# A gated mix of a long convolution and an MLP mixer: layer norm 2 as centred squares, full-height matmuls for the D term, and a new order

## The chip, the cores and the metric

The kernel runs on one core of a Trainium2 chip. The metric is the device time in microseconds (us) of one execution; the figure for a kernel is the median over its runs. A core has five engines with a program each: TensorE (PE, matmuls; its weight loads are listed as PEld), VectorE (DVE), ScalarE (ACT), GpSimd (POOL) and SyncE (SP, which here issues the DMAs). They run side by side and wait for one another through semaphores.

## The reference

With S = 2048 tokens, D = 640 and F = 1536, all in bfloat16, the output mixes two branches of the same input q:

```python
def reference(A_q, A_k, A_v, A_shift_k, A_ssm_k, A_ssm_D, B_x, B_w1, B_w2, B_w3, B_w4, gate_w):
    x = A_q
    g = sigmoid((x * gate_w).sum(-1, keepdims=True))
    # branch a: short convolution of k (4 taps), times v, long convolution over the sequence
    k_shift = sum_t k_pad[:, t:t + S, :] * shift_k[:, 3 - t]
    kv = k_shift * v
    y = irfft(rfft(kv, padded to 2 S) * rfft(ssm_k, padded to 2 S))[:S]     # per channel
    a = q * (y + kv * ssm_D)
    # branch b: two layer norms with an MLP each
    h = gelu(layernorm(x) @ w1)                 # layernorm: (x - mean) / sqrt(var + 1e-5)
    hs = (four column groups of h, shifted by 1, -1, 2, -2 tokens) @ w2
    x1 = x + hs
    b = x1 + gelu(layernorm(x1) @ w3) @ w4
    return g * a + (1 - g) * b
```

## The kernel before

The 2048 tokens are held as 16 slabs of 128 (partition p of slab t is token 16 p + t), and `QX[:, s, :]` holds slab s of q, later of x1, and at last of the output. Names of steps below are those of the plan, followed by slab or chunk numbers.

Branch b: `st0`, `rs0` and `xn0` are layer norm 1 (statistics, reciprocal root on GpSimd, normalised slab on VectorE). `xt` transposes a slab into `XNT` by DMA (`tr` does it by TensorE for the first slabs). `W1.c.n` is the first matmul for chunk c of four slabs (L586), `g1` its gelu on ScalarE (L593), `mx` the copies that shift the remainders of the column groups (L621 to L626). `W2.s` (L675) and `add s` (L682, VectorE) give x1; the add also sums each row into `SSM`. Layer norm 2 is `st1.s` (one square on ScalarE with a row sum into `SSQ`, L515), `rs1.s` on GpSimd for a pair of slabs (L531 to L535: mean, its square, subtraction, epsilon, power -0.5) and `xn1.s` on VectorE. `W3.c.f` (L761), `g2` (gelu, L765), `W4.s.j` (L774) and `w4e` (L780, VectorE) follow. The gate is `z` and `gate0` (VectorE), `gate1` (tanh on ScalarE, L648), `gate2`; `xo` scales x1 by 1 - g.

Branch a: the long convolution is done in two steps of a transform, through DRAM. Step 1 of the filter is `h1.s.h` (L730), evicted as `he` into staging and written by `hw` to `GHD`; the filter comes in as `h0` to `h4` and is transposed by `trh`. At slab 0 each of these two steps also adds the D term, the product of a row of ones and zeros (`ONE1`) with D (`DROW`), a matmul of one row (L733). `ka`, `kb`, `kc`, `k1` to `k3` load k and `v0` to `v3` load v (L807). VectorE forms kv by products (`km`, L823) and sums (`ka.`, L827), and `kv s` multiplies by v for two slabs (L830). `x1.s.h`, `xe`, `xw` are step 1 for kv, written to `GXD`. `rh` and `rx` read the two back in another order (L874), `h2` and `x2` are step 2 as 64-wide matmuls (L847), `sw` swaps real and imaginary parts (two DMAs), `pq` multiplies (L907, VectorE), `pv` transforms back, `vw` writes to `VD`, `rv` reads, `iv s` (L943) is the last step, `y` and `ya` form g * q * y and add it to `QX`, and `st s` stores a slab. `rq` loads q again.

`m3i`, `m3b`, `m3c`, `m3d`, `m3s`, `m3n` build the matrices of step 2: iotas and `m3c` (L444 to L460) on GpSimd, `m3d` (L464) on VectorE, the sine `m3s` (L466) on ScalarE, `m3n` on GpSimd.

The order of all the work is written out: `ORDER` is a text of 789 entries such as `W2.9/P/2`, which give a step, its engine (P TensorE, V VectorE, A ScalarE, G GpSimd, S SyncE's DMA queue) and the slots of the buffers it uses (banks of PSUM, staging areas). Each engine does its own entries in the order of the text. `Plan.add` takes for each step a time per engine; the text was made with them, and once it is written they have no effect on the program. PSUM has eight banks of 512 floats, and a step that needs a bank waits until the one before in that bank has been evicted.

Of the kernel before, what the change touches and what calls it, by code (L numbers as in the profile page):

```python
# [9 lines left out]
ACT = mybir.ActivationFunctionType  # L10
# [75 lines left out]
bpi/V is/G cs/V iw/G cw/V ang3/V and3/V sin3.1/A q1/S idn/G h0/S ang1/V ang2/V and1/V st0.2/V sin1.1/A abs1/A q0/S st0.1/A  # L86
st0.3/V warm/P/0 trh0/P/2 trhe0/A/2 h4/S trh4/P/4 st0.0/V ang0/V and0/V sin0.1/A h1/S trh1/P/6 trhe1/A/6 sin1.0/A rs0.2/G
xn0.2/V/0 xn0.3/V/1 tr0.0.2/P/0/0/0/1 trhe4/V/4 rs0.0/G misc/G xn0.1/V/2 xn0.0/V/0 h3/S trh3/P/2 abs0/A sin0.0/A and2/V
te0.0.2/V/0/0 sin2.1/A tr0.0.0/P/4/0/0/2 te0.0.0/V/4/0 q3/S st0.7/V st0.6/V w1/S W1.0.3/P/0/0 W1.0.2/P/1/0 w1m/G q2/S st0.4/A
trhe3/V/2 st0.5/V h2/S trh2/P/6 g1.0.3/A/0 g1.0.2/A/1 W1.0.0/P/2/0 g1.0.0/A/2 trhe2/V/6 W1.0.4/P/3/0 g1.0.4/A/3 h1.5.0/P/4/0  # L90
h1.1.1/P/6/1 he.1.1/A/6/1 rs0.6/G xn0.6/V/1 xn0.7/V/0 tr0.1.2/P/0/1/1/0 q7/S q4/S q5/S st0.10/A rs0.4/G xn0.4/V/2 q6/S gw/S
gt.0/P/2/0 w2b3/S he.5.0/V/4/0 h1.4.0/P/4/0 he.4.0/A/4/0 xn0.5/V/0 te0.1.2/V/0/1 tr0.1.0/P/6/1/2/0 te0.1.0/V/6/1 z0/V/2
h1.3.1/P/0/2 st0.11/V he.3.1/A/0/2 W1.0.1/P/3/0 h1.5.1/P/6/0 g1.0.1/A/3 w2b2/S he.5.1/A/6/0 h1.3.0/P/4/2 he.3.0/A/4/2
W1.1.4/P/2/1 h1.4.1/P/0/0 he.4.1/A/0/0 g1.1.4/A/2 W1.1.1/P/3/1 h1.1.0/P/6/1 g1.1.1/A/3 he.1.0/A/6/1 h1.2.1/P/4/2 he.2.1/A/4/2
w2b1/S w2a/S w2b0/S W1.1.2/P/2/1 drow/S kc/S/0 ka/S/0 h1.0.1/P/0/1 he.0.1/A/0/1 h1.0.0/P/6/1 he.0.0/A/6/1 cjb/S g1.1.2/A/2
W1.1.3/P/3/1 st0.9/V h1.2.0/P/4/2 he.2.0/A/4/2 g1.1.3/A/3 hw2/S/0 W1.1.0/P/0/1 g1.1.0/A/0 mx0.1/G rs0.10/G st0.8/V rs0.8/G
xn0.10/V/1 xt0.2.2/S/0/1 st0.15/V xn0.11/V/0 st0.14/V xt0.2.3/S/0/0 rs0.14/G mx0.2/V xn0.9/V/2 st0.12/V mx0.0/V mx1.3/G
st0.13/V gt.1/P/1/1 xn0.8/V/1 z1/V/1 hw0/S/1 xt0.2.1/S/0/2 h1.7.0/P/6/0 h1.7.1/P/4/0 v0/S he.7.0/V/6/0 xt0.2.0/S/0/1 abs3/A
xn0.15/V/0 xt0.3.3/S/1/0 W2.2/P/2 sin3.0/A add2/V/2 abs2/A he.7.1/A/4/0 h1.6.0/P/0/0 st1.2/A he.6.0/V/0/0 mx1.1/G W2.4/P/6
add4/V/6 sin2.0/A m3i1/G xn0.14/V/2 kb/S/0 hw1/S/2 W2.3/P/2 add3/V/2 h1.13.0/P/0/1 he.13.0/V/0/1 h1.6.1/P/4/0 he.6.1/A/4/0  # L100
rs0.12/G xt0.3.2/S/1/2 kz/V/0 xn0.12/V/1 xn0.13/V/0 mx1.0/G W2.5/P/6 hw3/S/0 xt0.3.1/S/1/0 xt0.3.0/S/1/1 add5/V/6 h1.12.1/P/2/1
gt.2/P/0/0 he.12.1/A/2/1 h1.12.0/P/4/1 he.12.0/V/4/1 W1.2.1/P/1/0 st1.4/A st1.3/A g1.2.1/A/1 m3i2/G m3i0/G m3i3/G mx1.2/G cj1/G
m3i5/G v1/S h1.13.1/P/2/1 he.13.1/V/2/1 mx0.3/G cj0/G hw6/S/1 W1.2.2/P/6/0 cj3/G z2/V/0 h1.8.1/P/4/2 he.8.1/A/4/2 m3i4/G
W1.2.4/P/0/0 st1.5/A W1.2.3/P/1/0 g1.2.3/A/1 h1.10.1/P/2/0 he.10.1/A/2/0 h1.10.0/P/4/0 he.10.0/A/4/0 g1.2.4/A/0 W1.2.0/P/7/0
g1.2.0/A/7 km0.0.3/V/0/0 h1.9.0/P/2/2 m3b/V he.9.0/A/2/2 g1.2.2/A/6 W1.3.0/P/1/1 h1.8.0/P/4/2 he.8.0/A/4/2 cj2/G km0.0.2/V/0/0
km0.0.1/V/0/1 ka0.0.2/V/0/0 rs1.2/G xn1.2/V/2 xt1.0.0/S/0/2 ka0.0.1/V/1/0 xn1.3/V/0 km0.0.0/V/0/0 gt.3/P/0/1 z3/V/0
ka0.0.0/V/0/0 kv0/V/0 h1.11.1/P/2/0 he.11.1/A/2/0 W1.3.1/P/6/1 g1.3.1/A/6 h1.9.1/P/4/2 he.9.1/A/4/2 g1.3.0/A/1 W1.3.3/P/0/1
h1.14.1/P/2/1 h1.15.0/P/6/1 he.15.0/A/6/1 he.14.1/A/2/1 h1.14.0/P/4/1 he.14.0/A/4/1 W1.3.4/P/1/1 g1.3.4/A/1 g1.3.3/A/0
W1.3.2/P/6/1 g1.3.2/A/6 w3/S h1.11.0/P/2/0 he.11.0/A/2/0 km0.1.3/V/0/0 rs1.4/G xn1.4/V/1 xt1.0.1/S/0/0 xt1.0.2/S/0/1 xn1.5/V/2
xt1.0.3/S/0/2 mx2.3/V gate0/V mx2.1/G W2.7/P/4 mx2.0/G km0.1.2/V/0/1 km0.1.1/V/0/0 ka0.1.2/V/1/0 ka0.1.1/V/0/0 m3c/G m3d/V  # L110
m3s/A m3n/G k1/S/1 mx2.2/G mx3.1/V km0.1.0/V/0/1 mx3.0/G ka0.1.0/V/1/0 W2.6/P/0 add6/V/0 add7/V/4 W2.8/P/6 add8/V/6 gate1/A
gate2/V kv2/V/0 W2.9/P/2 add9/V/2 km1.0.3/V/1/0 km1.0.2/V/1/0 km1.0.1/V/1/1 W3.0.1/P/0/0/0 g2.0.1/A/0/0 ka1.0.2/V/0/0 mx3.3/G
km1.0.0/V/1/0 ka1.0.1/V/1/0 ka1.0.0/V/0/0 kv4/V/0 xo5/A st1.6/A st1.8/A st1.9/A rs1.8/G xn1.9/V/0 k2/S/0 w4/S v2/S
km1.1.3/V/1/0 W3.0.4/P/1/0/1 W3.0.11/P/0/0/2 hw5/S/0 g2.0.11/A/0/2 g2.0.4/A/1/1 km1.1.2/V/1/1 ka1.1.2/V/1/0 xn1.8/V/1
km1.1.1/V/1/0 ka1.1.1/V/0/0 xt1.1.2/S/1/1 hw4/S/2 tri0/S xo2/V h1.15.1/P/4/1 v3/S km1.1.0/V/1/1 ka1.1.0/V/1/0 st1.7/A
he.15.1/A/4/1 rs1.6/G xn1.7/V/2 W3.0.6/P/2/0/1 W3.0.5/P/3/0/1 g2.0.5/A/3/1 g2.0.6/A/2/1 kv6/V/0 W2.11/P/6 W3.0.7/P/0/0/1
add11/V/6 xt1.1.1/S/1/2 km2.0.3/V/0/0 km2.0.2/V/0/0 W3.0.0/P/1/0/0 W3.0.8/P/2/0/2 g2.0.8/A/2/2 g2.0.0/A/1/0 xn1.6/V/1
xt1.1.0/S/1/1 xt1.1.3/S/1/0 W3.0.9/P/3/0/2 g2.0.9/A/3/2 xo4/A W3.0.3/P/2/0/0 W3.0.2/P/1/0/0 g2.0.7/A/0/1 g2.0.3/A/2/0 xo3/A
g2.0.2/A/1/0 ka2.0.2/V/0/0 W3.0.10/P/0/0/2 W2.10/P/4 km2.0.1/V/0/1 add10/V/4 ka2.0.1/V/1/0 km2.0.0/V/0/0 ka2.0.0/V/0/0 kv8/V/0
g2.0.10/A/0/2 W4.3.1/P/0/0/1/2 w4e3.1/V/0 W4.5.1/P/1/0/1/2 W4.5.0/P/2/0/1/2 W4.2.1/P/3/0/1/2 x1.2.0/P/6/0 W4.3.0/P/4/0/1/2  # L120
xe.2.0/A/6/0 km2.1.3/V/0/0 w4e3.0/V/4 km2.1.2/V/0/1 st1.11/A W2.13/P/6 w4e5.1/V/1 w4e2.1/V/3 W4.4.0/P/0/0/1/2 w4e5.0/V/2
W2.12/P/4 w4e4.0/V/0 add12/V/4 st1.10/A ka2.1.2/V/1/0 km2.1.1/V/0/0 W4.2.0/P/0/0/1/2 st1.12/A W3.1.10/P/1/1/3 w4e2.0/V/0
add13/V/6 km2.1.0/V/0/1 ka2.1.1/V/0/0 ka2.1.0/V/1/0 kv10/V/0 hw7/S/1 k3/S/1 tri1/S mx3.2/G rs1.10/G xn1.11/V/2 xt1.2.1/S/0/2
x1.3.1/P/2/0 xe.3.1/A/2/0 st1.13/A g2.1.10/A/1/3 rs1.12/G km3.0.3/V/1/0 km3.0.2/V/1/0 ka3.0.2/V/0/0 km3.0.1/V/1/1 x1.3.0/P/4/0
xe.3.0/A/4/0 W3.1.8/P/0/1/3 g2.1.8/A/0/3 xn1.13/V/1 ka3.0.1/V/1/0 km3.0.0/V/1/0 ka3.0.0/V/0/0 x1.2.1/P/6/0 xe.2.1/A/6/0
kv12/V/0 xw1/S/0 W4.4.1/P/2/0/1/2 w4e4.1/V/2 x1.0.1/P/4/2 xe.0.1/A/4/2 x1.0.0/P/0/2 xe.0.0/A/0/2 W3.1.1/P/3/1/0 g2.1.1/A/3/0
x1.6.1/P/6/1 xe.6.1/A/6/1 W3.1.7/P/0/1/1 g2.1.7/A/0/1 x1.1.1/P/4/2 x1.1.0/P/6/2 W3.1.9/P/1/1/3 xe.1.0/A/6/2 xe.1.1/A/4/2
x1.7.1/P/6/1 xe.7.1/A/6/1 g2.1.9/A/1/3 W3.1.0/P/0/1/0 g2.1.0/A/0/0 xt1.2.3/S/0/1 xw0/S/2 x1.7.0/P/4/1 xe.7.0/A/4/1 x1.6.0/P/6/1
xe.6.0/A/6/1 xw3/S/1 xn1.12/V/0 xn1.10/V/2 km3.1.3/V/1/0 xt1.2.0/S/0/2 xt1.2.2/S/0/0 W3.1.3/P/1/1/0 g2.1.3/A/1/0 km3.1.2/V/1/1
ka3.1.2/V/1/0 km3.1.1/V/1/0 xo12/V ka3.1.1/V/0/0 km3.1.0/V/1/1 ka3.1.0/V/1/0 kv14/V/0 x1.9.1/P/4/0 x1.8.0/P/2/0 xe.8.0/A/2/0  # L130
xe.9.1/A/4/0 W3.1.4/P/0/1/1 g2.1.4/A/0/1 x1.9.0/P/6/0 xe.9.0/A/6/0 W3.1.2/P/1/1/0 g2.1.2/A/1/0 x1.8.1/P/2/0 xe.8.1/A/2/0
xw4/S/0 x1.12.0/P/4/2 xe.12.0/A/4/2 x1.13.0/P/6/2 xe.13.0/A/6/2 W3.1.5/P/0/1/1 x1.13.1/P/2/2 xe.13.1/A/2/2 x1.12.1/P/4/2
xe.12.1/A/4/2 xw6/S/2 W3.1.11/P/1/1/3 g2.1.11/A/1/3 x1.10.1/P/6/1 x1.10.0/P/2/1 xe.10.0/V/2/1 xe.10.1/V/6/1 xo7/A W2.14/P/4
g2.1.5/A/0/1 W2.1/P/2 add14/V/4 rh0/S/0 x1.4.1/P/0/0 x1.5.1/P/6/0 xe.5.1/A/6/0 add1/V/2 W2.0/P/4 rh1/S/1 x1.15.0/P/2/2 st1.1/A
xe.15.0/A/2/2 add0/V/4 st1.0/A xe.4.1/V/0/0 W3.1.6/P/6/1/1 xo9/V rs1.0/G x1.11.1/P/4/1 xe.11.1/A/4/1 st1.14/A x1.4.0/P/2/0
W3.2.1/P/7/0/2 g2.2.1/A/7/2 xe.4.0/A/2/0 xo8/V x1.11.0/P/0/1 xe.11.0/V/0/1 xw5/S/1 W2.15/P/4 x1.14.0/P/0/2 xe.14.0/V/0/2
add15/V/4 x1.5.0/P/2/0 xe.5.0/A/2/0 xw2/S/0 W3.2.3/P/7/0/2 g2.1.6/A/6/1 xn1.0/V/1 x1.15.1/P/0/2 xe.15.1/V/0/2 g2.2.3/A/7/2
x1.14.1/P/2/2 xe.14.1/A/2/2 xw7/S/2 st1.15/A rs1.14/G xt1.3.2/S/1/1 rq0/S/0 W3.2.0/P/6/0/2 h2.1.1/P/4/1/0 h2e.1.1/A/4/0
g2.2.0/A/6/2 h2.1.4/P/2/1/0 h2e.1.4/V/2/0 h2.1.3/P/0/1/0 W3.2.2/P/7/0/2 h2e.1.3/V/0/0 h2.1.0/P/4/1/0 h2.0.3/P/2/0/1
h2e.0.3/A/2/1 h2e.1.0/V/4/0 g2.2.2/A/7/2 W4.8.1/P/6/0/1/3 h2.1.2/P/0/1/0 h2e.1.2/V/0/0 w4e8.1/V/6 h2.0.0/P/2/0/1 h2.0.1/P/4/0/1  # L140
# [39 lines left out]
def kernel(  # L180
# [322 lines left out]
    def ln_slab(i, s, dep):  # L503
        s0 = s & ~1

        def f_st(e):
# [4 lines left out]
            else:  # L511
                if i == 0:
                    nc.scalar.activation(out=JNK if i else JN0, in_=QX[:, s, :], func=ACT.Copy, scale=1.0 / D,
                                         accum_out=MV[:, i, s, 0:1])
# [485 lines left out]
```

## Time and profile before

| | us |
|---|---|
| median of 4 runs (lowest, highest) | 230.19 (229.45, 231.22) |
| the profiled execution's own time | 230.35 |
| its span | 228.6 |
| TensorE busy | 214.7 (94%) |
| VectorE busy | 189.7 (83%) |
| ScalarE busy | 162.6 (71%) |
| GpSimd busy | 62.1 (27%) |
| DMA: 65.90 MB | mean 288 GB/s |

The span is the time from the first to the last recorded piece of the execution; the rest of its time lies around it. The page also cuts the span into 40 slices of 5.7 us; each digit is the busy share in tenths (9 is 90% or more), and PEclk is the TensorE clock that was granted:

```profile
PE   6869999999789999999999999999989999999990
DVE  8998989989599999999976878888869887027993
ACT  5999979899677713199967863698982987616760
POOL 2653469699858403260002200000000000000000
PEclk9999999999979999999999999999999999999999
```

The chain that ended last is followed back from the last instruction: at each step to what released it, or to the instruction before on its engine. In a group's line stand the line of code, engine, operation, output and input, shapes, the count, then busy time and the mean in ns of one, then the idle time of the engine ahead of them and what ended most of it.

### The profile page before, as it was taken

To read this page: it belongs to the slowest core of one execution; us is meant where nothing else is said; L and a number is where in the kernel's file an instruction comes from. 1 tells how busy PE (TensorE), PEld (TensorE's weight loads), DVE (VectorE), ACT (ScalarE), POOL (GpSimd) and SP (SyncE) were. 2 spreads that over 40 slices of the span, in tenths; PEclk is the share of its full clock that TensorE was granted. 3 is DMA by queue.
4 is the path that set the end of the run, shared out by engine and by line. 5 is a ranking of instruction groups with operands and counts; after the bars stand their busy time and mean duration, and the time that the engine had idled before them with its cause. 6 is when DMAs were issued, how large, how long until landed. Compare 5 with 4: busy or idle time off the path is not lost.

```text
span 228.6 us, 4449 instructions
## 1 busy us (share of the span) xinstructions
PE 214.7 (94%) x1641; PEld 125.1 (55%) x1641; DVE 189.7 (83%) x347; ACT 162.6 (71%) x250; POOL 62.1 (27%) x133
## 2 busy tenths in 40 slices
PE   6869999999789999999999999999989999999990
PEld 6737557555535477655575456533335554457770
DVE  8998989989599999999976878888869887027993
ACT  5999979899677713199967863698982987616760
POOL 2653469699858403260002200000000000000000
PEclk9999999999979999999999999999999999999999
DMA  7999999999999499909999989999997973889985
GB/s 214 383 394 248 313 256 197 296 265 362 285 330 364 167 230 243 301 11 193 302 292 372 351 246 373 247 297 372 358 377 230 391 292 136 287 297 397 394 288 180
DMA packets 53030, 65.90 MB, mean 288 GB/s; under 512 B 22544, under 2 KB 39697, under 8 KB 52624
## 3 DMA queue, kind: packets, MB, share of 16 engines
q1 hardware_dynamic: 53008, 65.61, 92.5%
q8 instruction: 13, 0.21, 0.4%
q14 instruction: 9, 0.07, 0.1%
HBM read 37.03 MB, written 18.35 MB: 242 GB/s over the span
## 4 chain that ended last, share of the span: by engine, by line
PE 61%; DMA 12%; DVE 10%; POOL 7%; issue 3%; SPq 2%; ACT 1%; ACTq 0%; DVEq 0%; POOLq 0%
PE PS L774 18%; PE PS L761 16%; PE PS L675 7%; PE PS L847 6%; DMA RG<-in_A_ssm_k_dram 5%; PE PS L730 5%; DMA RK<-GHD 4%; PE PS L586 4%; PE PS L943 4%; DMA R<-R 3%; POOL MV L531 2%; DVE RK L827 2%; DVE RK L823 2%; DVE QX L682 1%; POOL RS L535 1%
## 5 line engine op out<-in xcount | busy, mean ns | idle before, releaser
L332 ACT CAST SX<-PS 128x640 bf16<-128x640 f32 (+1 forms) x65 | 47.7, 764 | 25.4 <-PE PS L730 13.3
L761 PE MATMUL PS<-XNT,W 128*128 128x512 bf16 x240 | 58.2, 388 | 2.1 <-DVE QX L682 2.1
L774 PE MATMUL PS<-W,RG 128*128 128x320 bf16 x384 | 56.0, 299 | 0.6 <-ACT RG L765 0.6
L774 PEld LDWEIGHTS <-RG 128*128 128x128 bf16 x384 | 36.5, 98 | 19.6 <-issue 4.7
L761 PEld LDWEIGHTS <-W 128*128 128x128 bf16 x240 | 23.1, 100 | 30.5 <-issue 8.5
L765 ACT ACTIVATE RG<-PS 128x512 bf16<-128x512 f32 x48 | 27.5, 604 | 6.6 <-PE PS L761 6.3
L907 DVE TENSOR_TENSOR SX<-SX,R 128x2048 bf16<-128x2048 bf16 x20 | 24.3, 1221 | 3.5 <-ACT SX L332 2.2
L780 DVE SCALAR_TENSOR_TENSOR QX<-PS,ZG,QX 128x320 bf16<-128x320 f32 x32 | 16.9, 545 | 11.1 <-PE PS L774 10.9
L586 PE MATMUL PS<-XNT,R 128*128 128x512 bf16 x100 | 24.2, 379 | 1.0 <-DMA R<-in_B_w_dram 1.0
L730 PE MATMUL PS<-KV,F 128*128 128x320 bf16 x128 | 24.9, 299 | 0.1
L675 PE MATMUL PS<-R 128*128 128x320 bf16 x160 | 23.5, 299 | 0.0
L336 DVE CAST SX<-PS 128x640 bf16<-128x640 f32 (+1 forms) x19 | 18.1, 966 | 3.5 <-PE PS L730 1.9
L827 DVE TENSOR_TENSOR RK<-RK 128x1280 bf16<-128x1280 bf16 x24 | 19.8, 826 | 0.4
L332 ACT CAST KV<-PS 128x1024 bf16<-128x1024 f32 x18 | 18.0, 1025 | 2.1 <-PE PS L847 2.0
L823 DVE TENSOR_TENSOR RK<-RK,CJ 128x1280 bf16<-128x1280 bf16 x24 | 19.4, 817 | 0.0
L675 PEld LDWEIGHTS <-R 128*128 128x128 bf16 x160 | 15.7, 98 | 6.4
L531 POOL TENSOR_SCALAR MV<-ST 128x2 f32<-128x2 f32 x8 | 7.2, 904 | 39.5 <-DVE QX L682 39.2
L730 PEld LDWEIGHTS <-F 128*128 128x128 bf16 x128 | 12.2, 98 | 9.7 <-issue 0.3
L586 PEld LDWEIGHTS <-R 128*128 128x128 bf16 x100 | 9.6, 98 | 10.5 <-DMA R<-in_B_w_dram 1.2
L515 ACT ACTIVATE RG<-QX 128x640 bf16<-128x640 bf16 x16 | 11.8, 737 | 4.7 <-issue 4.6
L682 DVE SCALAR_TENSOR_TENSOR QX<-PS,QX 128x640 bf16<-128x640 f32 x16 | 12.9, 818 | 2.4 <-PE PS L675 2.3
L847 PEld LDWEIGHTS <-M 64*64 64x64 bf16 x320 | 7.5, 105 | 12.9 <-issue 7.0
(110 smaller groups left out, 292.2 us busy)
## 6 DMA issues: line engine op xcount, KB each, us to landing
GHD<-SX SPq DMA_DIRECT2D x8, 640.0 KB, 4.6
GXD<-SX SPq DMA_DIRECT2D x8, 640.0 KB, 4.2
RK<-GHD SPq DMA_DIRECT2D x4, 1280.0 KB, 8.6
RK<-GXD SPq DMA_DIRECT2D x4, 1280.0 KB, 7.5
R<-R SPq DMA_DIRECT2D x8, 640.0 KB, 7.5
VD<-KV SPq DMA_DIRECT2D x4, 1280.0 KB, 7.2
W<-in_B_w_dram SPq DMA_DIRECT2D x2, 1920.0 KB, 9.5
RK<-in_A_k_dram SPq DMA_DIRECT2D x3, 1120.0 KB, 6.0
```

The source lines that it names most:

```text
L332: nc.scalar.copy(out=o, in_=i)
L336: nc.vector.tensor_copy(out=o, in_=i)
L586: nc.tensor.matmul(ps(pb), lhsT=lhsT, rhs=XNT[:, xb.idx, k, :], start=(k == 0), stop=(k == DT - 1))
L675: nc.tensor.matmul(ps(pb)[:, j, 0:DH], lhsT=gst_ap(k, s), rhs=W2[:, k, j * DH:(j + 1) * DH], start=(k == 0), stop=(k == DT - 1))
L730: nc.tensor.matmul(ps(pb)[:, j, 0:DH], lhsT=F1[:, s // 4, h, s % 4, :], rhs=src[:, s, ds], start=True, stop=not dterm)
L761: nc.tensor.matmul(ps(pb), lhsT=W3[:, k, f0 * P:(f0 + 1) * P], rhs=XNT[:, xb.idx, k, :], start=(k == 0), stop=(k == DT - 1))
L765: gns.append(pl.add("g2.%d.%d" % (c, f0), {A: act_p(512)}, lambda e, f0=f0, pb=pb, gb=gb: nc.scalar.activation(out=GTP[:, gb.idx, f0 % 4, ...
L774: nc.tensor.matmul(ps(pb)[:, 0:DH], lhsT=GTP[:, gbs[f // 4].idx, f % 4, i * P:(i + 1) * P], rhs=W4[:, f, j * DH:(j + 1) * DH], start=(f == ...
L823: m = pl.add("km%d.%d.%d" % (c, u, j), {V: dve(2 * D, .52)}, lambda e, src=src, cj=cj, tb=tb: nc.vector.tensor_tensor(out=TMP[:, tb.idx].r ...
L827: prev = pl.add("ka%d.%d.%d" % (c, u, j), {V: dve(2 * D, .52)}, lambda e, tb=tb: nc.vector.tensor_tensor(out=acc, in0=acc, in1=TMP[:, tb.i ...
L847: nc.tensor.matmul(pt[64 * C:64 * C + 64, R, :], lhsT=M3[64 * R:64 * R + 64, m, :], rhs=rhs_fn(R, C), start=start, stop=stop)
L907: nc.vector.tensor_tensor(out=PQ[:, qb.idx], in0=XS[:, sb.idx].unsqueeze(1).to_broadcast([P, 2, 1024]), in1=HH[:, hhb.idx, u], op=ALU.mult)
```

## The change

1. Layer norm 2: `st1.s` on ScalarE is now a copy of one column, `SSM * (-1/D)` into `MV` (the negated mean), and then a square of x1 with that as its bias and the row sum into `SSQ`. The second waits for the first. `rs1` on GpSimd is then two instructions in place of five, and `xn1` adds the negated mean instead of subtracting the mean.
2. The D term: `ONE1` becomes 128 x 128, zero except for its first row; `DROW` holds D on all 128 partitions, loaded by a broadcast (160 KB in place of 1.2 KB). The matmuls of L733 then have 128 rows.
3. Times of the plan: `m3c` 5000 to 7000 ns, `st1` 735 to 930, `rs1` 2300 to 1900, the first two `h1` doubled.
4. `ORDER` is another text throughout, with the same 789 steps: order on each engine, slots of buffers, and the engine of some (21 from VectorE to ScalarE and 16 the other way, nearly all evictions; `kz`, `mx0.0`, `mx2.3`, `mx3.1` from VectorE to GpSimd, `mx1.0` back). The table loads of ScalarE become eight, from seven: the gate's tanh now stands between gelus. Of the DMA queue: `v0` is issued after `xt0.3.0` (before: ahead of `xt0.2.0`), `rq0` after `rh2`, `rq1` and `rq2` late.

```diff
-    ONE1 = big.tile([1, P], BF16, name="ONE1")
+    ONE1 = big.tile([P, P], BF16, name="ONE1")
...
-    DROW = W34[0:1, 14700:14700 + D]
-    lddr = pl.dma("drow", lambda e: nc.sync.dma_start(out=DROW, in_=A_ssm_D.rearrange("(o d) -> o d", o=1)), D * 2, ldq, ndesc=1)
+    DROW = W34[:, 14700:14700 + D]
+    lddr = pl.dma("drow", lambda e: nc.sync.dma_start(out=DROW, in_=A_ssm_D.partition_broadcast(P)), P * D * 2, [ldq[-1]], ndesc=128)
...
-    m3c = pl.add("m3c", {G: 5000}, f_m3c, m3a)
+    m3c = pl.add("m3c", {G: 7000}, f_m3c, m3a)
...
         nc.gpsimd.memset(ONE1[:], 0.0)
-        nc.gpsimd.memset(ONE1.rearrange("p (j c) -> p j c", c=2)[:, :, 0:1], 1.0)
+        nc.gpsimd.memset(ONE1[0:1, :].rearrange("p (j c) -> p j c", c=2)[:, :, 0:1], 1.0)
...
+                else:
+                    nc.scalar.activation(out=MV[:, i, s, 0:1], in_=SSM[:, s:s + 1], func=ACT.Copy, scale=-1.0 / D)
+                    nc.scalar.activation(out=JNK, in_=QX[:, s, :], func=ACT.Square, bias=MV[:, i, s, 0:1],
+                                         accum_out=SSQ[:, s:s + 1])
...
+                if i == 1:
+                    ve = VE[:, i, s0:s0 + 2]
+                    g.tensor_scalar(out=ve, in0=SSQ[:, s0:s0 + 2], scalar1=1.0 / D, scalar2=1e-5, op0=ALU.mult, op1=ALU.add)
+                    g.tensor_tensor(out=RS[:, i, s0:s0 + 2], in0=ve, in1=NHALF[:], op=ALU.pow)
+                    return
...
-                        if i == 1:
-                            g.tensor_scalar(out=m[:, :, 0], in0=SSM[:, a:b], scalar1=1.0 / D, scalar2=None, op0=ALU.mult)
...
-            op0=ALU.subtract, op1=ALU.mult), [rsn[(i, s0)]], [b])
+            op0=ALU.subtract if i == 0 else ALU.add, op1=ALU.mult), [rsn[(i, s0)]], [b])
```

Of the 90 lines of `ORDER`, those that hold `v0`, `gate1`, `m3c`, `kv14` and `rx0`:

```diff
-st0.13/V gt.1/P/1/1 xn0.8/V/1 z1/V/1 hw0/S/1 xt0.2.1/S/0/2 h1.7.0/P/6/0 h1.7.1/P/4/0 v0/S he.7.0/V/6/0 xt0.2.0/S/0/1 abs3/A
...
-xt1.0.3/S/0/2 mx2.3/V gate0/V mx2.1/G W2.7/P/4 mx2.0/G km0.1.2/V/0/1 km0.1.1/V/0/0 ka0.1.2/V/1/0 ka0.1.1/V/0/0 m3c/G m3d/V
-m3s/A m3n/G k1/S/1 mx2.2/G mx3.1/V km0.1.0/V/0/1 mx3.0/G ka0.1.0/V/1/0 W2.6/P/0 add6/V/0 add7/V/4 W2.8/P/6 add8/V/6 gate1/A
...
-ka3.1.2/V/1/0 km3.1.1/V/1/0 xo12/V ka3.1.1/V/0/0 km3.1.0/V/1/1 ka3.1.0/V/1/0 kv14/V/0 x1.9.1/P/4/0 x1.8.0/P/2/0 xe.8.0/A/2/0
...
-w4e9.1/V/7 W4.7.1/P/6/0/1/3 w4e7.1/V/6 W4.9.0/P/0/0/1/3 w4e9.0/V/0 xn1.14/V/0 xo14/V W4.8.0/P/1/0/1/3 w4e8.0/V/1 rx0/S/1
...
+xt0.3.0/S/1/1 W1.2.4/P/6/0 gt.2/P/7/0 g1.2.4/A/6 v0/S W2.5/P/4 z2/V/7 add5/V/4 h1.13.0/P/0/1 he.13.0/A/0/1 W1.2.2/P/7/0 cj3/G
...
+h1.10.1/P/4/2 he.10.1/V/4/2 W1.3.2/P/7/1 h1.9.0/P/2/1 W1.3.4/P/0/1 gate1/A he.9.0/A/2/1 g1.2.0/A/6 h1.8.0/P/4/1 he.8.0/A/4/1
...
+W2.9/P/0 add9/V/0 h1.10.0/P/2/2 W2.8/P/6 add8/V/6 h1.14.0/P/4/0 he.14.0/A/4/0 m3c/G m3d/V m3s/A m3n/G ka0.1.1/V/0/0 st1.9/A
...
+x1.13.0/P/6/2 x1.12.0/P/4/2 xe.13.0/A/6/2 xe.12.0/A/4/2 xw6/S/2 ka3.1.1/V/0/0 ka3.1.0/V/1/0 kv14/V/0 rh1/S/0 rh0/S/1
...
+h2e.0.4/A/6/1 rx0/S/0 W4.9.0/P/2/1/0/3 w4e9.0/V/2 W4.7.1/P/3/1/0/3 w4e7.1/V/3 W4.8.0/P/0/1/0/3 w4e8.0/V/0 x2.0.4/P/6/0/0
```

## The prediction

> **What bounds the kernel now.** I read the page's first lines, then the chain that ended last, then TensorE's waits, and then windows around the two places where these meet.
>
> ```profile
> span 228.6 us, 4449 instructions
> ...
> PE 214.7 (94%) x1641; PEld 125.1 (55%) x1641; DVE 189.7 (83%) x347; ACT 162.6 (71%) x250; POOL 62.1 (27%) x133
> ...
> PE 61%; DMA 12%; DVE 10%; POOL 7%; issue 3%; SPq 2%; ACT 1%; ACTq 0%; DVEq 0%; POOLq 0%
> ```
>
> TensorE is busy for 94% of the span, so the time is TensorE's work plus the few places where it stands still. VectorE has little room, ScalarE some, GpSimd much, yet 7% of the chain runs over GpSimd. The chain shows where:
>
> ```profile
> 28.87 0.14 PE PS L730
> 29.01 0.24 PE PS L733
> 29.25 0.24 PE PS L730
> ...
> 45.42 4.12 POOL MV L531
> ...
> 50.48 1.24 POOL RS L535
> ...
> 60.20 0.35 POOL W L459
> ...
> 60.58 0.27 DVE W L464
> 60.88 0.46 ACT W L466
> 61.35 1.28 ACT L648
> 62.65 0.22 ACT ZG L648
> 62.87 0.82 DVE QX L682 x2
> 63.73 5.08 PE PS L761 x15
> 68.82 0.27 PE PS L730 x2
> ```
>
> A `rs1` (layer norm 2, L531 to L535) holds GpSimd from 45.4 to 51.7; behind it run copies and `m3c` (L444 to L460), until 60.5; VectorE stands at `m3d` (L464), and with it the adds (L682) that free PSUM for TensorE, which starts again at 63.73. Of TensorE's waits, by releaser and with the longest at the end, that one is the largest:
>
> ```profile
> PE PS L761 <- DVE QX L682: 2.1, 1, 2.1
> PE PS L847 <- DMA RK<-GHD: 0.9, 2, 0.7
> PE PS L774 <- ACT RG L765: 0.6, 1, 0.6
> ```
>
> After it TensorE works at a lower clock. In this window of five microseconds (columns: length, PE, weight loads, VectorE, ScalarE, GpSimd, granted clock, DMA share, GB/s) the clock is 0.70, against 1.00 in its neighbours:
>
> ```profile
> 65.00:70.00 5.00, 5.00 (x18) 2.05 (x17) 4.93 (x13) 4.46 (x11) 2.15 (x5) 0.70 1.00 373
> ```
>
> The 15 matmuls from 63.73 are three groups that take 1.08 each elsewhere, 3.24; they took 5.08. So this stop cost 2.1 + 1.84 = 3.95 us.
>
> TensorE's time lost after the last transpose of the filter (16.9) is then 3.95 here, 0.3 at `x1.8.0`, 0.2 at `pv.1.3`, 0.2 at `h2.2.2`, 0.85 at `h2.3.1` (both L847, waiting for `rh2` and `rh3`) and 0.65 at `W4.0.0`: 6.2 us. Its last matmul ends at 223.3; without the lost time it would be 217.1. From there to the end of the span are 5.3 (eviction, store), and outside the span 1.8 (230.35 - 228.56). The profiled execution stands 0.16 above the median of 230.19.
>
> **The change, part by part.**
>
> *D term.* In the chain, full-height matmuls (L730) and one-row ones (L733) alternate 0.24 apart, eight in a row, 1.9 us; the pair of L730 alone at 68.82 took 0.27. Eight at 0.135 are 1.1: 0.7 to 0.8 us less, all of it on TensorE. Bounds: 0 if the 0.24 belongs to something other than the height, 0.8 as taken. The row is weighed against two rules: the Trainium skill, TensorEngine Tiling (Array Packing), Key Properties, says that a change of tiling mode drains TensorE, which would explain 0.24; TensorE: Matmul & The Clock Gate, Why this matters for your kernels, says that a K=32 matmul takes as long as a K=128 one, by which the gain would be 0. The load of D grows from 1.2 to 160 KB: at the rate of the 640 KB loads of v (5.2 us) 1.3 us of queue; in the new order it is issued some 10 us ahead of `h1.0.1` (25.7), so that covers it, and if not it costs up to 1.3. The zeroing of 128 rows instead of one (L474, as large, took 0.28) lies in GpSimd's early idle time.
>
> *GpSimd's part of layer norm 2.* Five instructions become two. By the groups
>
> ```profile
> L531 POOL TENSOR_SCALAR MV<-ST 128x2 f32<-128x2 f32 x8 | 7.2, 904 | 39.5 <-DVE QX L682 39.2
> L532 POOL TENSOR_TENSOR ST<-MV 128x2 f32<-128x2 f32 x8 | 4.1, 514 | 0.7
> L534 POOL TENSOR_SCALAR VE<-VE 128x2 f32<-128x2 f32 x8 | 3.6, 446 | 0.7
> ```
>
> and L533 (359 ns), eight pairs lose 8 x 2.22 = 17.8 us and gain one L534 each, 3.6: 14.2 us of GpSimd less. GpSimd is busy for 27%, so this counts only at 45 to 61, where a single L531 took 4.12, ahead of `m3c`. VectorE was running two-input products back to back then. The Trainium skill, SBUF — State Buffer, Who interferes with whom, has VectorE and GpSimd excluding each other for whole instructions; by that the remaining two instructions can be held up as L531 was, once each.
>
> *ScalarE's part.* Each of 16 slabs gets a 128x1 copy ahead of its square, and a wait of ScalarE for its own result. No row has this; the nearest is L648 (128x16), 215 ns. I take 0.3 with the wait, bounds 0.2 (the row alone) and 0.45 (row plus a gap as long again): 4.8 us on ScalarE, 3.2 to 7.2. At 71% busy most of it lies beside TensorE; what is queued behind are the gelu evictions that free PSUM banks. Four of the 16, `st1.2` to `st1.5`, come ahead of the W2 to W3 change; 1.2 us of my stalls there are theirs. The tanh of the gate now stands between gelus and costs one more table load: rows of 1.28 each, two in succession around it.
>
> *The order.* The whole table is new, and it decides more than the arithmetic. I went along each engine's new order with the durations and pitches of the profile's rows (W1 and W3 1.08, W2 1.36, W4 1.63, a pair of L730 0.27, h2 0.235, iv 0.545), and looked at each crossing for who is late:
> - `m3d`: `rs1.4` ends on GpSimd near 48.4, and `m3c` (6.9 in the chain) with what lies ahead of it near 56.5. VectorE has its own 9.6 us between the first `kv` and `m3d`, which brings it there at 58. The stall of 3.95 goes.
> - The four steps that go to GpSimd cost it 0.4 to 0.9 each (L621's forms; `kz` as the slowest). `mx2.3` alone stands ahead of `m3c`, and is in the 56.5; were it as slow as 1.1, the slower piece of L621 in the chain, there is still a microsecond left. The evictions that change places between ScalarE (701 ns for 640 columns, L332) and VectorE (818, L336) leave the sums within 3 us. The plan's longer times issue nothing: they cost nothing, on any path.
> - In its place are smaller ones by 61: 0.2 at `W1.1.0`; 0.6 at `W1.2.4`, whose last transposed slab lands at about 39, against 38.4 on TensorE; 0.6 at `W1.3.0` and 1.3 at `W2.9`, both for evictions behind the two table loads. Together 2.7.
> - `v0` is moved behind the transposes of slabs 12 to 15 and is issued at 44 instead of 33.77; 5.2 later is 49.2, and `kv0` wants it at 48.6. VectorE absorbs 0.6.
> - `kv14` then ends at 113.7 (115.7 before), and `rh0`, `rh1` behind it land 11.1 later, at 124.8, against 125.3 for `h2.0.3`: covered by half a microsecond. `rq0` to `rq2` no longer stand ahead of `rx0`, `rh2` and `rh3`; the losses of 0.2 and 0.85 there go. `rx0` comes out at 137.5 for a need at 137.
> - At the end `vw3` lands for `rv0` at 200, in time; `iv5` waits some 0.6 for `rv2`.
> - Last matmul to end of span: 5.3 as before, since both close with `W4.0.1`, its eviction and one store.
>
> Sum: 217.1 - 0.7 + 2.7 + 0.6 = 219.7; with 5.3 the span is 225.0, with 1.8 outside 226.8, and 226.6 against the median.
>
> **Rivals.**
> - *v0 comes late* (slower). It is issued behind four transposes and ahead of the writes of the filter and W3, while the DMA share is at 1.0. A load of the same size, `v2`, took 11.3 (63.90 to 75.23). At 11.3 `kv0` starts at 55.3 instead of 49.2, and `kv14` ends 6.1 later, near 120; `rh1` lands at 131, 5.5 after TensorE wants it, and the time is 232. It turns to slower than before when `kv14` ends after 119; from 114.2 on TensorE pays one for one. For it: no slack in VectorE (83%, and 90% or more in those slices). Against: the median of 5.2.
> - *The stall only moves* (about the same). If ScalarE's new work and the table loads make `W2.9` wait over two microseconds, the low clock returns with it: another 1.3 + 1.8, 229.7. For it: 2.1 idle was enough before. Against: my four stalls are short and apart.
> - *No new stall* (faster than forecast). All evictions come in time: 217.1 - 0.7 + 5.3 + 1.8 = 223.5.
> - *The D term saves nothing*: 227.3, inside the forecast's range.
>
> **How the numbers follow.** The measurement tells about 0.5% from no change, 229.0 to 231.3. Chances: forecast, 225 to 228.5, 0.50; no new stall 0.13; the stall moves 0.17, a third of it below 229.0; v0 late, or `kv14` late by another way, 0.20, nearly all above 231.3. So faster 0.50 + 0.13 + 0.05 = 0.68, same 0.12, slower 0.20. The range runs from 223.2 (no stall, and ScalarE's wait at its lower bound) to 231.6, leaving out half of the last case and little else; the forecast's own is 225 to 228.5.
>
> **What would show it.** Right: the pair at `h1.0.0` without steps of 0.24; no wait of VectorE on GpSimd at `m3d`; clock at 1.00 from 60 to 70; GpSimd's sum down by about 14 us, ScalarE's up by 5 to 7; `kv14` ending by 114; the last matmul near 219.7. Wrong: a wait of TensorE over 2 us anywhere after 17, with a low clock behind it; VectorE idle on v; `h2.0.3` or `x2.0.4` waiting for their loads; ScalarE's pairs of copy and square over 1.3 us.

## The result and the profile after

The changed kernel is not faster but slightly slower: the ratio of its times to those before is 1.0036 (95% interval 1.0021 to 1.0052). Ratios here leave out executions more than 1.5% above the fastest of their kernel (12 of the changed kernel's 36), and the profile after is of one of these (232.93 us), so a second profile of the same kernel (229.27 us, below) is set beside it. Over all runs the medians are 231.25 us (36 runs, 228.82 to 236.06) and 229.79 (57 runs, 229.01 to 232.16); the changed kernel scatters more, and part of what follows is why. The forecast was 226.6.

One sentence of the description of the change was wrong, and a step of the prediction rests on it: the table loads of ScalarE do not become eight. The profile before has seven, the profile after six. The number of entries of `ORDER` was wrong too, but nothing rests on it: there are 942, not 789.

The page of the changed kernel, its first lines and the shares of the chain:

```profile
span 231.1 us, 4420 instructions
...
PE 214.4 (93%) x1641; PEld 125.5 (54%) x1641; DVE 188.8 (82%) x339; ACT 170.2 (74%) x270; POOL 51.3 (22%) x112
...
PE 41%; DVE 34%; DMA 15%; issue 6%; SPq 1%; ACT 1%; DVEq 0%
```

GpSimd lost 10.8 us of work and is out of the chain. TensorE has as much work as before. VectorE's share of the chain went from 10% to 34%, with less work than before (188.8 against 189.7). So the chain now runs over VectorE; in the second profile its share is 28%, and TensorE's 49%. The chain of the profile after shows to where (stretch 84 to 93 us; start, duration, piece):

```profile
86.04 0.92 DVE QX L786 x2
86.96 0.73 DVE RK L833
87.69 0.47 DVE QX L786
88.16 0.04 issue
88.20 3.02 PE PS L780 x12
```

L786 is the eviction `w4e` of a W4 result (L780 before), L833 a sum of the short convolution (L827 before), and L780 is now the W4 matmul (L774 before). VectorE evicts two W4 results (the first two of L786), does one sum, and then the eviction that frees the bank for `W4.4.0`. TensorE stood for 2.3 us until then, and the twelve matmuls, 1.63 elsewhere, took 3.02, at a low clock (shown below).

### The profile page after: what moved, and what is told of

It reads as the page before. It is cut to its first block, busy times and chain, and to the rows that moved or that the text cites. A ratio compares the mean times of both kernels' runs of the same rounds, so it can differ in the third digit from the quotient of the medians.

```text
span 231.1 us, 4420 instructions
## 1 busy us (share of the span) xinstructions
PE 214.4 (93%) x1641; PEld 125.5 (54%) x1641; DVE 188.8 (82%) x339; ACT 170.2 (74%) x270; POOL 51.3 (22%) x112
## 4 chain that ended last, share of the span: by engine, by line
PE 41%; DVE 34%; DMA 15%; issue 6%; SPq 1%; ACT 1%; DVEq 0%
PE PS L780 12%; PE PS L767 10%; DVE RK L829 7%; PE PS L853 6%; DVE RK L833 6%; PE PS L681 5%; DMA GWT<-in_gate_w_dram 4%; DMA R<-R 4%; PE PS L736 4%; DMA RG<-in_A_ssm_k_dram 3%; DMA RK<-VD 3%; PE PS L592 3%; DVE XN L548 3%; DVE QX L969 2%; DVE QX L688 2%
## 5 line engine op out<-in xcount | busy, mean ns | idle before, releaser
L332 ACT CAST SX<-PS 128x640 bf16<-128x640 f32 (+1 forms) x69 | 51.8, 776 | 27.1 <-PE PS L736 17.0
L780 PE MATMUL PS<-W,RG 128*128 128x320 bf16 x384 | 57.3, 304 | 2.3 <-DVE QX L786 2.3
L767 PE MATMUL PS<-XNT,W 128*128 128x512 bf16 x240 | 56.0, 379 | 0.0
L780 PEld LDWEIGHTS <-RG 128*128 128x128 bf16 x384 | 37.1, 99 | 21.8 <-issue 7.4
L786 DVE SCALAR_TENSOR_TENSOR QX<-PS,ZG,QX 128x320 bf16<-128x320 f32 x32 | 16.8, 546 | 16.5 <-PE PS L780 16.4
L736 PE MATMUL PS<-KV,F 128*128 128x320 bf16 x128 | 25.8, 304 | 0.9 <-DVE ZG L615 0.5
L829 DVE TENSOR_TENSOR RK<-RK,CJ 128x1280 bf16<-128x1280 bf16 x24 | 21.0, 880 | 0.0
L833 DVE TENSOR_TENSOR RK<-RK 128x1280 bf16<-128x1280 bf16 x24 | 20.6, 857 | 0.5
L548 DVE TENSOR_SCALAR XN<-QX,MV,RS 128x640 bf16<-128x640 bf16 x32 | 15.4, 503 | 1.4 <-POOL RS L541 0.9
L527 POOL TENSOR_SCALAR VE<-ST 128x2 f32<-128x2 f32 x8 | 3.3, 413 | 59.0 <-ACT RG L518 36.7
L338 DVE TENSOR_SCALAR R<-PS 128x1024 bf16<-128x1024 f32 x10 | 11.9, 1219 | 4.9 <-PE PS L853 4.9
L336 DVE CAST SX<-PS 128x640 bf16<-128x640 f32 (+1 forms) x15 | 13.3, 899 | 2.8 <-PE PS L853 1.1
```

What stands on the lines that cost most here:

```text
L332: nc.scalar.copy(out=o, in_=i)
L548: xn = pl.add("xn%d.%d" % (i, s), {V: 360}, lambda e: nc.vector.tensor_scalar(out=XN[:, b.idx, :], in0=QX[:, s, :], scalar1=MV[:, i, s, 0: ...
L736: nc.tensor.matmul(ps(pb)[:, j, 0:DH], lhsT=F1[:, s // 4, h, s % 4, :], rhs=src[:, s, ds], start=True, stop=not dterm)
L767: nc.tensor.matmul(ps(pb), lhsT=W3[:, k, f0 * P:(f0 + 1) * P], rhs=XNT[:, xb.idx, k, :], start=(k == 0), stop=(k == DT - 1))
L780: nc.tensor.matmul(ps(pb)[:, 0:DH], lhsT=GTP[:, gbs[f // 4].idx, f % 4, i * P:(i + 1) * P], rhs=W4[:, f, j * DH:(j + 1) * DH], start=(f == ...
L829: m = pl.add("km%d.%d.%d" % (c, u, j), {V: dve(2 * D, .52)}, lambda e, src=src, cj=cj, tb=tb: nc.vector.tensor_tensor(out=TMP[:, tb.idx].r ...
```

## The experiments

Runs of one group were timed beside the kernel before on the same chip; ratios are to it. The groups ran on three chips, so kernels of different groups are compared by their ratios.

**The changed kernel again.**

> The changed kernel once more, beside the others of this group. Theory (VectorE): in the new order GpSimd's mx copies fall on VectorE's km and ka products and sums (0.82 each alone, 1.08 to 1.25 beside a copy), VectorE comes late to the eviction w4e2.0, TensorE stands at W4.4.0 for about 2.3 us and then works at a lower clock. This run should show that wait again, between 1.5 and 3, and kv14 ending between 116 and 119; time 230 to 231.5. Rival (ScalarE): the extra copies of layer norm 2 and the extra table load cost the time, so that TensorE's waits would be on ScalarE's evictions.

Measured: ratio 1.0045 (1.0008 to 1.0081), median 230.95, runs from 228.82 to 236.06. Its profiled execution (229.27, span 227.4) is the second profile, the one that the prediction's sums are held against below. TensorE's waits in it begin with

```profile
PE PS L780 <- DVE QX L786: 2.3, 1, 2.3
```

the same wait at the same place, 2.27 us, and `kv14` ends at 117.3. TensorE's longest wait for ScalarE is 0.8. The windows around it, first of the profile after, then of this one (two microseconds each; the clock is the figure after the five engines):

```profile
88.00:90.00 2.00, 1.80 (x9) 1.10 (x9) 2.00 (x5) 0.00 (x0) 0.00 (x0) 0.65 0.81 298
90.00:92.00 2.00, 2.00 (x9) 1.16 (x8) 1.65 (x4) 0.00 (x0) 0.00 (x0) 0.50 1.23 172
```

```profile
88.00:90.00 2.00, 1.24 (x10) 0.89 (x10) 2.00 (x6) 0.00 (x0) 0.00 (x0) 1.00 0.81 263
90.00:92.00 2.00, 2.00 (x17) 1.45 (x15) 1.97 (x4) 0.87 (x2) 0.00 (x0) 1.00 1.15 208
```

The same program stood for the same 2.27 us in both executions; after it the clock was 0.65 and 0.50 with 18 matmuls in four microseconds in the first, and 1.00 with 27 matmuls in the second. The stop itself cost the same in both; the low clock came behind it in one of the two. By the starts of TensorE's steps the second part cost 1.7 us in the first of these two. The clock is only part of the scatter: over the 37 executions behind the result the time goes with the mean granted clock (correlation -0.70), but at a mean clock of 1.00 the times still run from 228.82 to 231.21.

**The new order with the old code.** The `ORDER` of the changed kernel, all other lines of the kernel before.

> The new order with layer norm 2 and the D term as before (five GpSimd instructions, one square, one-row matmuls). Rival (ScalarE): without the 16 small copies it is faster than the changed kernel by 1 to 3 us, 228 to 229.5. Theory (VectorE): the old rs1 loads GpSimd more and holds m3c and xn1 up, the D term costs 0.7: slower than the changed kernel by 1 to 3 us, 231.5 to 234.

Measured: 1.0100 (1.0056 to 1.0145), median 232.42. The new code does not cost the time: in the same order the old code is slower (the interval overlaps that of the twelve runs above, but lies above 1.0021 to 1.0052, that of the 36). The rival with ScalarE falls. The wait at `W4.4.0` is 2.5 here, and the clock behind it is low again, 0.60 and 0.54 from 90 to 94 us.

**The old order with the new code.** The `ORDER` of the kernel before, all other lines of the changed kernel.

> The order of before with both new pieces of code (centred squares on ScalarE with the short rs1, full-height D term). Theory (VectorE; the code gains, the new order loses): the rs1 of slabs 4 and 5 takes 1.5 to 2 us on GpSimd in place of 6.3, m3c ends 3 to 4 us sooner, the wait of 2.1 us at the change from W2 to W3 goes and the clock stays up: 225.8 to 227.5. Rival (ScalarE): 16 small copies cost TensorE more than that, 229.8 or above.

Measured: 0.9952 (0.9928 to 0.9975), median 228.81. The sign is the theory's, the size (1.1 us, where 2.4 to 4.1 were expected) is about a third. The change is thus a gain in its code (0.5%) and a loss in its order (about 0.9%, 1.0045 against 0.9952; 1.0% with the old code). The chain and TensorE's waits of this kernel tell why the gain is small:

```profile
47.10 0.20 ACT RG L518
...
47.38 2.19 POOL VE L527
...
52.16 0.76 POOL W L444
...
53.16 0.83 POOL W L446
...
59.84 0.35 POOL W L459
...
60.22 0.27 DVE W L464
```

```profile
PE PS L767 <- DVE QX L688: 1.0, 1, 1.0
```

`rs1` has two instructions instead of five, but three things took most of that back. It starts 2.0 us later (47.38, where L531 had started at 45.42): its first instruction now needs ScalarE's square (L518, the line above it), and before only the third did. That first instruction (L527) then took 2.19 us, where its group's mean in the changed kernel is 0.41. And `m3c` (L444 to L459) ran from 52.2 to 60.2 where it had run from 53.6 to 60.55, 1.1 us longer: L444, L446 and one L458 took 0.76, 0.83 and 0.77 in place of 0.26, 0.32 and 0.32. So GpSimd got less to do and finished 0.35 us earlier. TensorE's wait shrank from 2.1 to 1.0, and the clock stayed at 1.00. The expectation that a shorter `rs1` would bring `m3c` forward by 3 to 4 us was wrong.

**The old order with the D term alone.**

```diff
-    ONE1 = big.tile([1, P], BF16, name="ONE1")
+    ONE1 = big.tile([P, P], BF16, name="ONE1")
...
-    DROW = W34[0:1, 14700:14700 + D]
+    DROW = W34[:, 14700:14700 + D]
```

(with its load and the row of ones as in the change)

> The order of before with the full-height D term alone. Both theories: the eight matmuls at h1.0 take 1.1 us in place of 1.9, TensorE is 0.7 to 0.8 us earlier from there on; of this 0.4 to 0.8 arrives at the end if the waits at m3d and at rh2 and rh3 do not take it back, so 229.0 to 229.5; no change if VectorE's wait at m3d, which hangs on GpSimd, takes it all.

Measured: 0.9984 (0.9956 to 1.0013), median 229.59. The chain at `h1.0` (the first four of eight):

```profile
29.39 0.14 PE PS L730
29.52 0.14 PE PS L733
29.66 0.14 PE PS L730
29.79 0.14 PE PS L733
```

0.135 apart in place of 0.24: the eight matmuls take 1.08 instead of 1.9, which answers the question of height. Of the 0.8 us, what arrives at the end cannot be told from nothing here. In its profile a new wait of 0.4 at a W2 (for an eviction by VectorE) and the old 2.0 at `m3d` stand behind it.

**The evictions ahead of five products and sums.** The changed kernel; in `ORDER` five steps of VectorE are moved down, past `w4e4.1` (parts of lines):

```diff
-xo4/V km2.0.2/V/0/0 ka2.0.2/V/0/0 km2.0.1/V/0/1 km2.0.0/V/0/0 xn1.9/V/1
+xo4/V xn1.9/V/1
...
-xe.3.1/A/6/1 ka2.0.1/V/1/0 xt1.1.1/S/1/0
+xe.3.1/A/6/1 xt1.1.1/S/1/0
...
-w4e2.0/V/2 w4e4.1/V/3
+w4e2.0/V/2 w4e4.1/V/3 km2.0.2/V/0/0 ka2.0.2/V/0/0 km2.0.1/V/0/1 km2.0.0/V/0/0 ka2.0.1/V/1/0
```

> The changed kernel with five of VectorE's products and sums (km2.0.2 to ka2.0.1) put behind the W4 evictions w4e5.0, w4e3.1, w4e2.0 and w4e4.1; nothing else moves. Theory (the wait at W4.4.0 and the low clock that follows it in some executions are what the new order lost): w4e2.0 ends by 86.4 and TensorE does not stand at W4.4.0; VectorE does not wait for TensorE behind it either, so kv14 ends near 115; 226.0 to 228.0, and a smaller spread than the 228.8 to 236.1 of the changed kernel. Rival (VectorE's sum of work is the bound, the wait only changes its place): TensorE waits 2 us elsewhere before 130, 229.5 or above.

Measured: 0.9952 (0.9925 to 0.9979), median 228.61, runs from 227.85 to 230.25. `w4e2.0` ends at 84.4 in place of 88.7, `kv14` at 115.5 in place of 117.3. VectorE does the same work; only what TensorE waits for comes first. TensorE does not stand from 85 to 90, and the clock is full:

```profile
85.00:90.00 5.00, 5.00 (x39) 3.60 (x38) 4.97 (x8) 2.16 (x4) 0.00 (x0) 1.00 1.17 280
```

The ratio falls by 0.93%, some 2.1 us, from 1.0045 to 0.9952, which is also that of the new code in the old order: the whole loss of the new order is gone, and it is about as long as the wait itself (2.27). The runs lie within 2.4 us, in place of 7.2. The wait at `W4.4.0`, with the low clock behind it in some executions, is thus what the new order lost. The rival falls: the longest wait of TensorE after 18 us is 0.7. 228.61 is still above the expected range of 226.0 to 228.0; TensorE waits some 4 us in pieces of 0.2 to 0.7 there, but that these are the difference is not shown.

**Three copies on ScalarE.** The changed kernel, with `mx2.2`, `mx3.1` and `mx3.3` on ScalarE:

```diff
-W3.0.5/P/2/0/1 mx2.2/G mx3.1/G mx3.3/G W2.10/P/4
+W3.0.5/P/2/0/1 mx2.2/A mx3.1/A mx3.3/A W2.10/P/4
...
-                g = nc.gpsimd if e == G else nc.vector
+                cp = nc.scalar.copy if e == A else (nc.gpsimd if e == G else nc.vector).tensor_copy
...
```

> The changed kernel with the three copies mx2.2, mx3.1 and mx3.3 (GpSimd, 73 to 76 us) done by ScalarE. Theory (GpSimd's copies are what slows VectorE): km1.1.2, ka1.1.2 and km1.1.1 fall from 1.11 to 1.25 us to 0.82, w4e2.0 comes 1.1 us sooner, the wait at W4.4.0 is 1.0 to 1.4 in place of 2.3; 229 to 230. Rival (the transposing DMA tri1, which is issued at 73 too, slows them): they stay at 1.1 to 1.25 and the wait at 2.3.

Measured: 1.0018 (0.9983 to 1.0054), median 230.24. VectorE's timeline, first in the changed kernel's second profile with GpSimd's line below it, then here:

```profile
73.41 1.24 DVE L829 TENSOR_TENSOR RK<-RK,CJ 128x1280 bf16<-128x1280 bf16 x1
74.69 1.11 DVE L833 TENSOR_TENSOR RK<-RK 128x1280 bf16<-128x1280 bf16 x1
75.73 1.23 DVE L829 TENSOR_TENSOR RK<-RK,CJ 128x1280 bf16<-128x1280 bf16 x1
...
73.37 2.91 POOL L627 COPY R<-R 32x512 bf16<-32x512 bf16 x3
```

```profile
73.21 0.82 DVE L829 TENSOR_TENSOR RK<-RK,CJ 128x1280 bf16<-128x1280 bf16 x1
74.07 0.82 DVE L833 TENSOR_TENSOR RK<-RK 128x1280 bf16<-128x1280 bf16 x1
74.81 0.82 DVE L829 TENSOR_TENSOR RK<-RK,CJ 128x1280 bf16<-128x1280 bf16 x1
```

The three take 0.82 each without the copies, and 1.11 to 1.24 beside them. The rival with the transposing DMA falls: `tri1` is issued at the same place in both. `w4e2.0` ends 1.1 us earlier (87.6), and TensorE's wait is 0.8 in place of 2.3. TensorE comes 0.4 later itself, as a W2 waits for one of the copies on ScalarE. So GpSimd's three copies account for about half of that wait (1.1 of 2.3). The time lies between those of the changed kernel and of the kernel before, and cannot be told from either.

**Both moves on the changed kernel.**

> The changed kernel with both moves: the four W4 evictions ahead of five products and sums on VectorE, and mx2.2, mx3.1 and mx3.3 on ScalarE. If VectorE's delay by GpSimd's copies costs only through the wait at W4.4.0, which the first move has taken away, this gives the same as the first move alone, 228.2 to 229.0. If VectorE is the bound of the stretch up to kv14 in any case, the 1.1 us of VectorE arrive at kv14 and at the end: 227.3 to 228.0.

Measured: 0.9959 (0.9933 to 0.9985), median 229.12, not to be told from the first move alone (0.9952). The 1.1 us that VectorE loses beside these three copies cost through that one wait, and with the evictions first they cost nothing that can be measured. The expected 228.2 to 229.0 was missed by 0.1. Its runs go from 227.4 to 232.3, so the wait at `W4.4.0` is not the only source of scatter in this order; what the other is stays open.

**m3d behind the adds, in the old order.** The old order with the new code; `m3d`, `m3s`, `m3n` behind `add7`, `gate1` ahead of `m3s`, `mx2.2` and `mx3.0` ahead of `m3n` (parts of lines):

```diff
-ka0.1.1/V/0/0 m3c/G m3d/V m3s/A m3n/G k1/S/1 mx2.2/G mx3.1/V km0.1.0/V/0/1 mx3.0/G ka0.1.0/V/1/0 W2.6/P/0 add6/V/0 add7/V/4 W2.8/P/6 add8/V/6 gate1/A
+ka0.1.1/V/0/0 m3c/G gate1/A k1/S/1 mx3.1/V mx2.2/G mx3.0/G km0.1.0/V/0/1 ka0.1.0/V/1/0 W2.6/P/0 add6/V/0 add7/V/4 m3d/V m3s/A m3n/G W2.8/P/6 add8/V/6
```

> The order of before with both new pieces of code, and m3d, m3s and m3n put behind the adds add6 and add7, gate1 ahead of m3s, and mx2.2 and mx3.0 ahead of m3n. Theory (VectorE standing at m3d still holds TensorE up by 1.0 us in that kernel): no wait at W3.0.1 beyond 0.3, 227.2 to 228.3. Rival (another late step takes its place: g2.0.1 behind three table loads, or the second h2): 228.6 to 229.2 as without the move.

Measured: 0.9905 (0.9874 to 0.9936), median 227.79: the fastest of all kernels here, and faster than both the kernel before and the changed one. VectorE no longer keeps TensorE waiting at `W3.0.1`, but 1.0 us comes back as the rival had it, at the third W3 (65.26), for a gelu eviction behind ScalarE's table load:

```profile
PE PS L769 <- ACT RG L773: 1.2, 2, 1.0
```

**The same with two copies on ScalarE.** `mx2.2` and `mx3.0` on ScalarE, where the kernel above has it idle ahead of `m3s`.

> The order of before with both new pieces of code and m3d behind the adds, and mx2.2 and mx3.0 on ScalarE, which stands idle there for 3.4 us ahead of m3s. If GpSimd's copies slow VectorE here too, km0.1.0, ka0.1.0 and the adds get faster by 0.3 to 0.6 us together, m3n comes sooner and the wait of 1.0 us for g2.0.1 shrinks: 227.0 to 227.8. If the wait for g2.0.1 behind ScalarE's table load is all that is left, nothing changes: 227.6 to 228.0.

Measured: 0.9922 (0.9893 to 0.9951), median 228.04: no change. TensorE no longer waits for the gelu, but at the first W3 (62.45), for a transposed slab, and just as long:

```profile
PE PS L769 <- DMA XNT<-XN: 1.0, 1, 1.0
```

In the kernel above this W3 had started without a wait, at 62.0. So one wait went and another of the same length came at an earlier place; why the slab lands later here is not known.

## Why the prediction was wrong

The numbers are those of the second profile of the changed kernel (span 227.4, own time 229.3), unless another is named.

*The sum.* Forecast for the end of the last matmul 219.7; it ended at 222.3 there, and at 225.4 in the profile after. The 5.3 behind it were 5.1 and 5.7. Of the 2.6 us between forecast and second profile, 2.27 are the wait at `W4.4.0`, which the sum did not have.

*The D term*: right on TensorE. 0.24 fell to 0.135 apart, and the load of D landed at 23.8, 3 us ahead of its use. That the 0.7 us reach the end is not shown (0.9984, with 1 in its interval).

*GpSimd's part*: the size of `rs1` was right, its effect was not (see the old order with the new code). By the groups

```profile
L527 POOL TENSOR_SCALAR VE<-ST 128x2 f32<-128x2 f32 x8 | 3.3, 412 | 57.3 <-ACT RG L518 36.7 <-ACT MV L517 20.4
...
L518 ACT ACTIVATE RG<-QX,MV 128x640 bf16<-128x640 bf16 x16 | 13.3, 828 | 0.6
L517 ACT ACTIVATE MV<-ST 128x1 f32<-128x1 f32 x16 | 3.2, 200 | 2.2 <-DVE QX L688 2.1
```

eight pairs lose 17.8 us and gain 3.3. Yet the busy time fell by only 10.7, where 14.2 were forecast, as GpSimd also got two more copies on balance and the zeroing `kz`, and its copies of 32x512 took 847 ns each in place of 678.

*ScalarE's part*: its size was right. A copy of one column takes 200 ns, and the square with the mean as bias 828 in place of 737: 0.29 per slab, where 0.3 was taken. In the old order ScalarE's busy time rose by 3.8 us (162.5 to 166.3, with the D term in both), beside TensorE. In the changed kernel it rose by 7.4, where 5 to 7 were forecast. That `rs1` now waits for the square from its first instruction on was not in the forecast.

*The table load*: wrong. `gate1` stands between gelus and needs no load:

```profile
L410 ACT ACT_TABLE_LOAD x2 | 2.6, 1283 | 0.7 <-PEq L990 0.7
L599 ACT ACT_TABLE_LOAD x2 | 2.6, 1283 | 0.0
L466 ACT ACT_TABLE_LOAD x1 | 1.3, 1283 | 0.0
L771 ACT ACT_TABLE_LOAD x1 | 1.3, 1283 | 0.0
```

None of L654, the tanh; before, it had one, when it came behind the sine. The stalls that the forecast hung on it, 0.6 at `W1.3.0` and 1.3 at `W2.9`, did not come, nor did those at `W1.1.0` and `W1.2.4`. In their place TensorE waited 0.8 at `gt.0` for ScalarE, and for VectorE 0.7 at `W2.2` and 0.5 in `h1.9.0` (for `z3`), which were not foreseen. That the total from 17 us up to the first W3 came out (2.3 against 2.7) was luck.

*The order, `m3d`*: the stall went as forecast, though not at the times forecast. The part of `m3c` that `m3d` waits for (up to L459) ended at 59.1 instead of 56.5, and VectorE, late as well, came to `m3d` at 61.2 instead of 58, without a wait; the clock stayed at 1.00 from 60 to 70. That both were late by about 3 us and the margin stayed was luck.

*The order, VectorE behind it*: this is the step that failed. The prediction took VectorE's durations from the kernel before, and it priced the copies that go to GpSimd on GpSimd alone ("0.4 to 0.9 each"); what they cost VectorE it put at nothing, though for `rs1` it had reckoned with the opposite, VectorE holding GpSimd up. Products and sums, before and then in the second profile:

```profile
L827 DVE TENSOR_TENSOR RK<-RK 128x1280 bf16<-128x1280 bf16 x24 | 19.8, 826 | 0.4
L823 DVE TENSOR_TENSOR RK<-RK,CJ 128x1280 bf16<-128x1280 bf16 x24 | 19.4, 817 | 0.0
```

```profile
L829 DVE TENSOR_TENSOR RK<-RK,CJ 128x1280 bf16<-128x1280 bf16 x24 | 21.0, 880 | 0.0
L833 DVE TENSOR_TENSOR RK<-RK 128x1280 bf16<-128x1280 bf16 x24 | 20.6, 857 | 0.5
```

Over the 56 of them (the lines show 48, eight more stand in another line of code) the time above 0.82 each adds up to 0.3 us before and 2.6 in the new order. The twelve that take 0.87 or more all have a GpSimd instruction beside them, nine of them an `mx` copy, and three were back at 0.82 when their copies were taken away. The normalising step (L548) rose from 452 ns to 504 on the mean as well; one of them took 1.43 beside GpSimd's copies.

`kv0` had been placed at 49.2; it started at 51.9, straight behind VectorE's work and not behind `v0`, which had landed at 51.1. Step by step, against the median of steps of the same kind before, VectorE's work takes 2.7 us longer from 17 to `kv0` and 1.6 longer from there to `kv8`. An estimate from these: without them the eviction `w4e2.0` would have ended near 84.4 instead of 88.7, and TensorE came for its bank at 86.5. So there were 2.1 us of room, and this crossing was not on the list; with 4.3 us of error TensorE stood for 2.27 at `W4.4.0`. The mistake is one of method too: VectorE was placed from one anchor and its sum was never held against the 83% at which it had no room.

*The rest*: `kv14` ended at 117.3, 3.6 late, but `h2.0.3` and `x2.0.4` went with TensorE, not with their loads. `iv5` waited 0.64, where 0.6 was forecast.

*The rivals*: the one that came was "the stall only moves", with 229.7 against the measured 231.25. It had the mechanism, 2 us of standing and then the low clock, but at the wrong place and engine: VectorE at `W4.4.0` instead of ScalarE at `W2.9`. Of the fall-back to a low clock the prediction knew one instance and treated it as certain; behind this stop it came in one of the two profiled executions, and that adds to the scatter. The rival with `v0` did not come: its load took 5.1 us, as forecast.

The range ended at 231.6 and held the time; but the chance of 0.68 for faster rested on durations that the new neighbours on the other engine changed.

## What to carry to other kernels

A new order is a change in its own right, and here it cost about twice what the code beside it gained; timing old code in the new order and new code in the old one separates the two in two runs. On an engine that is nearly full, put what another engine waits for next ahead of work that is wanted later: letting four evictions go ahead of five products and sums won some 2.1 us without removing any work. Durations taken from another order hold only as long as the same engines run side by side.

## What the runs showed of the hardware

- A product or sum of two SBUF operands on VectorE (128x1280, bfloat16) takes 0.82 us alone and 1.11 to 1.24 beside a GpSimd copy, and GpSimd is held up in turn: the same tensor_scalar (L457) took 0.39 and 1.62 us in one kernel (the old order with the new code). The Trainium skill, SBUF — State Buffer, Who interferes with whom, has a VectorE instruction with two SBUF inputs contend with a GpSimd instruction that reads SBUF, and the loser wait; the traces agree. What had not been expected is that less work on GpSimd did not end sooner: in the old order the instructions of `rs1` ahead of the power took 4.9 us in place of 17.8, and `m3c` finished only 0.35 us earlier, in part because `rs1` started later.
- After a stop of TensorE of 2.27 us the granted clock was 0.65 and then 0.50 in one execution and 1.00 in another of the same program; after the 2.5 us of the old code in the new order it was 0.60 and 0.54, after the 2.1 us before the change 0.70 over five microseconds, and after the stop of 1.0 us in the old order with the new code it stayed at 1.00. The Trainium skill, TensorE: Matmul & The Clock Gate, Part 1, names an idle window of about 3.4 us for the fall to half rate; here stops of two thirds of that were enough at times.
- A tanh right behind a gelu on ScalarE needed no table load; behind a sine it needed one of 1.28 us.
